# Attention scores of two heads on 64 rows of the array each, in a fused attention and mixture-of-experts kernel

## The chip, the cores and the metric

One core of one Trainium2 chip runs the whole program. The metric is device time in microseconds (us). A profile is one execution; its span runs from the first to the last instruction.

## The reference

Block-causal attention (batch 4, 8 heads, 576 positions, head size 64, blocks of 64), and then four dense experts over the 2304 tokens:

```python
scores = scale * np.matmul(q, k.transpose(0, 1, 3, 2))
scores = np.where(block_i >= block_j, scores, -1000000000.0)   # blocks of 64
attn = np.exp(scores - np.max(scores, axis=-1, keepdims=True))
attn = attn / (np.sum(attn, axis=-1, keepdims=True) + 1e-09)
x = np.matmul(attn, v)             # then (B, S, H * D) as 2304 x 512
...
for e in range(E):                 # E = 4, w1[e] 512 x 1024, w2[e] 1024 x 512
    h = np.maximum(x @ w1[e], 0.0)
    out += p[:, e:e + 1] * (h @ w2[e])
```

## The kernel before, in words

**The experts.** The tokens are in five blocks: the first 64 positions of the four batches (256 tokens), and then positions 64 to 576 of each batch (512 tokens each). A block takes 32 chunks (expert, 128 hidden columns); a chunk is 12 products `h` (`mm1`, L961) and 6 or 12 products `acc` (`mm2`, L1006). All are fp32r products; each fp32 operand is split into a rounded high part and the low rest (`w1h` and `w1l`, `xh` and `xl`, `hh` and `hl`), and three products (high by high, high by low, low by high) stand for one.

**The attention** of batches 0 to 3 runs ahead of their blocks in units of two heads (`unit`). The four units of batch 0 are "plain": fp32 products of whole K and Q (L510), each head on its own 64 rows of the array. The twelve units of batches 1 to 3 are "split" units. In one of these K of both heads is transposed (`kT`), and for each head `KK` gets the high part on 64 partitions and the low part on the other 64 (two copies and two differences, with the columns rotated for the second head, so that the corner's stand side by side). Q is loaded twice, once for each half of the partitions, side by side for the heads (1024 columns), transposed (`qT`), and split into `HH` and `LL`. One product of `KK` with `HH` (L522) and one with `LL` (L523) then contract over all 128 rows, for every piece of keys: 512, 448, 320 and 192 query columns per head, and a corner of 64 keys for both heads together (L568, L569, 128 columns).

The products of a piece go to a PSUM tile `att` of 512 columns, of which there are two. They are emptied by a copy to `S` and running maxima into `cm`; GpSimd finds the maxima over the keys (`mx`), ScalarE takes exp, and `S` is split into `PH` and `PL` for the products with V (L723), of which the corner's (`VJ`) is fp32.

**The order** of all instructions is made while the program is built: `Flow.run` plays threads of operations against estimated costs, and takes the operation that can start first. `late` adds 1500 ns (`LAG`) to what a score product waits for. Expert products fill what is free on TensorE.

Of the kernel before, what the change touches and what calls it, by code (L numbers as in the profile page):

```python
# [206 lines left out]
def kernel(  # L207
# [60 lines left out]
    bufs("qr", 1, [P, 2 * MAXW])  # L268
    bufs("vr", 1, [P, MAXT, 2, D])
    bufs("kT", 1, [P, S])  # L270
    bufs("qT", 1, [P, 2 * MAXW])
    bufs("KK", 2, [P, 2 * S], F32R)
    bufs("HH", 1, [P, 2 * MAXW], F32R)
    bufs("LL", 1, [P, 2 * MAXW], F32R)
    bufs("VS", 2, [P, MAXT, 4, D], F32R)
    bufs("VJ", 2, [P, 2, 3, D])
# [24 lines left out]
    bufs("st", 4, [P, 32])  # L301
    ident = const.tile([P, P], F32, name="ident")
# [67 lines left out]
    def unit(u, ua, us, ju, pu, ph, job, dst, c):  # L370
# [13 lines left out]
        def k_thread():  # L384
# [33 lines left out]
        def q_thread():  # L418
            yield ("until", lambda: now[0] >= gate[u])
            yield ("until", lambda: started())  # L420
            qr = yield fl.take("qr", ua)
            vals = []
            for h, j in ((h, j) for h in range(2) for j in range(2 if plain else 4)):
                p0, c0 = (64 * h + 32 * j, 0) if plain else (32 * j, h * W)
                vals.append((yield dma(
                    qr.tile[p0:p0 + 32, c0:c0 + W].rearrange("c (i r) -> c i r", r=32),
                    q[b, h0 + h, q0:q1, 32 * (j % 2):32 * (j % 2) + 32].rearrange("(i c) r -> c i r", c=32),
                    W * 128, u=[qr], prio=pr)))
            yield ("until", lambda: left_first[0] == 0)
            qT = yield fl.take("qT", ua)  # L430
            n = W if plain else 2 * W
            t = yield op("dve", 1.04 * n + 70, lambda _: nc.vector.transpose(out=qT.tile[:, :n], in_=qr.tile[:, :n]),
                         vals, [qr, qT], pr)
            fl.give(qr)
            if plain:
                st["q"] = (qT, t)
                return
            HH = yield fl.take("HH", us)
            LL = yield fl.take("LL", us)
            a = yield a_copy(HH.tile[:, :2 * W], qT.tile[:, :2 * W], 2 * W, [t], [qT, HH], pr)  # L440
            l = yield tt(BOTH, LL.tile[:, :2 * W], qT.tile[:, :2 * W], HH.tile[:, :2 * W], SUB, 2 * W, [a], [qT, HH, LL], pr)
            fl.give(qT)
            st["q"] = (HH, LL, a, l)

        def v_thread():
# [12 lines left out]
            for h in range(2):  # L458
                if odd:
                    jv.append((yield dma(VJ.tile[64 * h:64 * h + 64, VJ.tile.shape[1] - 1, 1, :], v[b, h0 + h, q1 - MASK_BLOCK:q1], 64 * 256,  # L460
                                         u=[VJ], prio=pr + 0.005)))
# [26 lines left out]
        if plain:  # L488
            banks.sort(key=lambda x: (x[1][0][0], x[0]))
# [3 lines left out]
        def s_thread():  # L493
# [8 lines left out]
            if plain:  # L502
                qT, qv = st["q"]
                Q = [qT]
                need = lambda h: ka + [qv]
                cost = lambda w: 2 * max(107.0, 2 * w / 2.4 + 2.5)

                def product(o, h, k0, n, lo):
                    hp = slice(64 * h, 64 * h + 64)
                    nc.tensor.matmul(out=o, lhsT=KK.tile[hp, k0:k0 + n], rhs=qT.tile[hp, lo:W], start=True, stop=True)  # L510
            else:
                HH, LL, qa, ql = st["q"]
                Q = [HH, LL]
                Hv = HH.tile[:, :2 * W].rearrange("p (h w) -> p h w", h=2)
                Lv = LL.tile[:, :2 * W].rearrange("p (h w) -> p h w", h=2)
                need = lambda h: (ka + kb if h is None else kb if h else ka) + [qa, ql]
                cost = lambda w: 2 * max(85.0, w / 2.4 + PEO)

                def product(o, h, k0, n, lo):
                    at = k0 + (q1 + MASK_BLOCK * odd) * h  # L520
                    hs = h
                    nc.tensor.matmul(out=o, lhsT=KK.tile[:, at:at + n], rhs=Hv[:, hs, lo:W], start=True, stop=False)  # L522
                    nc.tensor.matmul(out=o, lhsT=KK.tile[:, at:at + n], rhs=Lv[:, hs, lo:W], start=False, stop=True)  # L523

            for h, ps_list in banks:
                if plain and h is not None:

                    if h:
                        continue
                    two = []  # L530
                    for _ in range(2):
                        two.append((yield fl.take("att", None, bank_tag)))

                    def fn(_, two=two, ps_list=ps_list):
                        at = 0
                        for j, a, w, _ in ps_list:
                            for g in range(2):
                                product(two[g].tile[:, at:at + w], g, P * j, P, a - q0)
                            at += w

                    ws = [x[2] for x in ps_list]
                    m = yield op("pe", 300.0 + (2 * sum(ws) + ws[0] - sum(abs(x - y) for x, y in zip(ws, ws[1:]))) / 1.2,
                                 fn, need(0), [*two, KK] + Q, pr)
                    for g in range(2):
                        done, at = [m], 0
                        for j, a, w, _ in ps_list:
                            if a == P * j:
                                done.append((yield op("dve", 75.0, lambda _, ps=two[g].tile, x=at: nc.vector.memset(
                                    ps[64:128, x:x + 64], neg), [m], [two[g]], pr)))
                            at += w  # L550
                        st["banks"].append((g, ps_list, two[g], done))
                    continue
                pb = yield fl.take("att", None, bank_tag)
                ps = pb.tile
                use = [pb, KK] + Q
                done = []
                if h is None:
                    lo = W - MASK_BLOCK
                    n = 2 * MASK_BLOCK

                    def fn(_, ps=ps, n=n, lo=lo):
                        if plain:
                            for g in range(2):
                                r = slice(64 * g, 64 * g + 64)
                                product(ps[r, r], g, q1 - MASK_BLOCK, MASK_BLOCK, lo)
                        else:
                            lhsT = KK.tile[:, q1 - MASK_BLOCK:q1 + MASK_BLOCK]
                            nc.tensor.matmul(out=ps[:, :n], lhsT=lhsT, rhs=Hv[:, :, lo:W], start=True, stop=False)  # L568
                            nc.tensor.matmul(out=ps[:, :n], lhsT=lhsT, rhs=Lv[:, :, lo:W], start=False, stop=True)  # L569

                    m = yield late(op("pe", 220.0, fn, need(None), use, pr), lag)
                    m1 = yield op("dve", 75.0, lambda _, ps=ps: nc.vector.memset(ps[64:128, 0:64], neg), [m], [pb], pr)
                    m2 = yield op("dve", 75.0, lambda _, ps=ps: nc.vector.memset(ps[0:64, 64:128], neg), [m], [pb], pr)
                    done = [m, m1, m2]
                else:
                    at = 0
                    corners = []
                    for j, a, w, _ in ps_list:

                        def fn(_, o=ps[:, at:at + w], j=j, h=h, a=a):  # L580
                            product(o, h, P * j, P, a - q0)

                        m = yield late(op("pe", cost(w), fn, need(h), use, pr), lag)
                        done = [m]
                        if a == P * j:
                            corners.append(at)
                        at += w
                    for x in corners:
                        done.append((yield op("dve", 75.0, lambda _, ps=ps, x=x: nc.vector.memset(ps[64:128, x:x + 64], neg),  # L589
                                              done[:1], [pb], pr)))  # L590
                st["banks"].append((h, ps_list, pb, done))
            fl.give(KK, *Q)

# [535 lines left out]
```

## Time and profile before

| | us |
|---|---|
| median of 3 runs (935.1 to 936.45) | 935.82 |
| the profiled execution | 934.92 |
| its span | 933.1 |
| TensorE (PE) busy | 922.1 |
| VectorE (DVE) busy | 727.8 |
| ScalarE (ACT) busy | 424.2 |
| GpSimd (POOL) busy | 140.6 |

The span leaves out 1.8 us of the execution's own time. PE is TensorE's matmuls and PEld its weight loads, which run beside them. A matmul's time in a row reaches to its modelled end, and matmuls are pipelined, so the cost of one in a stream is the step from its start to the start of the next. The chain that ended last gives such steps.

### The profile page before, as it was taken

The page shows a single profiled execution, that of the slowest core. Times are in us where ns is not written, and L with a number is a line of the kernel's source. Part 1 is how long each engine was busy: PE and PEld are TensorE (multiplying, and loading weights), DVE is VectorE, ACT ScalarE, POOL GpSimd, SP SyncE. Part 2 cuts the span into 40 slices and gives each one's busy share as a digit, 9 for nine tenths or more (in the row PEclk, how much of TensorE's full clock was granted, in tenths as well). Part 3 has the DMA queues.
Part 4 walks back from the last instruction along what each step waited for, and adds up shares of the span by engine and source line. Part 5 has one row for each costly group of instructions (what it writes and reads, how often), then busy time and mean ns, then how long its engine had stood idle before and what let it go on. Part 6 is the DMA issues. An engine that isn't in the chain of part 4 may idle for free.

```text
span 933.1 us, 12703 instructions
## 1 busy us (share of the span) xinstructions
PE 922.1 (99%) x4381; PEld 759.0 (81%) x4382; DVE 727.8 (78%) x1323; ACT 424.2 (45%) x726; POOL 140.6 (15%) x59
## 2 busy tenths in 40 slices
PE   8999999999999999999999999999999999999998
PEld 4777787888888888888888888888888888888886
DVE  6888879788998988878998889898987754545442
ACT  3477656645565445436454545454434322222220
POOL 2101100131212121212122202112121200000000
PEclk9999999999999999999999999999999999999999
DMA  9765447625352355452523546343523343333311
GB/s 167 169 172 149 125 144 177 160 69 138 89 133 77 102 131 152 97 128 79 142 69 99 127 125 161 100 107 113 116 84 88 99 148 98 95 101 92 100 57 45
DMA packets 235648, 107.83 MB, mean 116 GB/s; under 512 B 130880, under 2 KB 212800, under 8 KB 235584
## 3 DMA queue, kind: packets, MB, share of 16 engines
q1 hardware_dynamic: 232416, 106.24, 43.0%
q10 hardware_dynamic: 3168, 0.79, 0.5%
q8 instruction: 34, 0.56, 0.3%
q14 instruction: 30, 0.25, 0.1%
HBM read 102.27 MB, written 4.72 MB: 115 GB/s over the span
## 4 chain that ended last, share of the span: by engine, by line
PE 94%; DVE 2%; DMA 2%; ACT 1%; SPq 1%; issue 1%; DVEq 0%; ACTq 0%
PE h L961 42%; PE acc L1006 41%; PE att L723 5%; PE att L523 2%; PE att L522 2%; PE acc L723 1%; SPq L320 1%; DMA S<-in_k_dram 0%; DMA w2r<-in_moe_w_dram 0%; PE att L510 0%; DVE cm L333 0%; DMA kr<-in_k_dram 0%; DMA w1r<-in_moe_w_dram 0%; DVE o L1035 0%; PE acc L510 0%
## 5 line engine op out<-in xcount | busy, mean ns | idle before, releaser
L961 PE MATMUL h<-xh,w1h 128*128 128x512 f32 (+1 forms) x640 | 239.1, 374 | 0.6 <-ACT w1h L326 0.6
L961 PE MATMUL h<-xh,w1l 128*128 128x512 f32 (+1 forms) x640 | 236.1, 369 | 1.4 <-DVE w1l L333 1.4
L961 PE MATMUL h<-xl,w1h 128*128 128x512 f32 (+1 forms) x640 | 235.7, 368 | 0.0
L1006 PE MATMUL acc<-w2h,hh 128*128 128x512 f32 x576 | 226.3, 393 | 0.0
L1006 PE MATMUL acc<-w2l,hh 128*128 128x512 f32 x576 | 224.8, 390 | 0.0
L1006 PE MATMUL acc<-w2h,hl 128*128 128x512 f32 x576 | 224.5, 390 | 0.0
L978 ACT ACTIVATE hh<-h 128x512 fp32r<-128x512 f32 (+1 forms) x160 | 88.9, 556 | 206.9 <-PE h L961 204.1
L326 ACT CAST w2h<-w2r 128x512 fp32r<-128x512 f32 x153 | 95.1, 621 | 151.7 <-PE acc L1006 149.1
L333 DVE TENSOR_TENSOR w2l<-w2r,w2h 128x512 fp32r<-128x512 f32 x160 | 109.8, 686 | 53.3 <-ACT w2h L326 52.9
L961 PEld LDWEIGHTS h<-xh,w1h 128*128 128x128 f32 x640 | 120.7, 189 | 22.9 <-issue 2.2
L961 PEld LDWEIGHTS h<-xh,w1l 128*128 128x128 f32 x640 | 120.5, 188 | 22.3 <-DVE w1l L333 2.0
L961 PEld LDWEIGHTS h<-xl,w1h 128*128 128x128 f32 x640 | 120.7, 189 | 19.5 <-DVE xl L333 0.2
L980 DVE SCALAR_TENSOR_TENSOR hl<-h,hh 128x512 fp32r<-128x512 f32 (+1 forms) x160 | 100.8, 630 | 36.4 <-ACT hh L978 35.4
L1006 PEld LDWEIGHTS acc<-w2h,hl 128*128 128x128 f32 x576 | 108.2, 188 | 22.9
L1006 PEld LDWEIGHTS acc<-w2h,hh 128*128 128x128 f32 x576 | 108.3, 188 | 21.2 <-ACT w2h L326 0.7
L1006 PEld LDWEIGHTS acc<-w2l,hh 128*128 128x128 f32 x576 | 108.4, 188 | 20.1
L333 DVE TENSOR_TENSOR w1l<-w1r,w1h 128x512 fp32r<-128x512 f32 x160 | 114.4, 715 | 9.6 <-ACT w1h L326 5.9
L680 POOL PARTITION_ALL_REDUCE S<-S x24 | 81.3, 3437 | 240.2 <-DVE S L333 174.0
L644 POOL PARTITION_ALL_REDUCE mx<-cm x16 | 54.5, 3407 | 358.5 <-DVE cm L333 279.3
L326 ACT CAST w1h<-w1r 128x512 fp32r<-128x512 f32 x115 | 71.2, 619 | 16.7 <-DMA w1r<-in_moe_w_dram 16.4
L326 ACT COPY S<-att 128x512 f32<-128x512 f32 (+2 forms) x88 | 47.5, 540 | 54.5 <-DVE att L589 31.9
L333 DVE TENSOR_TENSOR S<-S,mx 128x1024 f32<-128x1024 f32 (+4 forms) x80 | 60.3, 791 | 4.0 <-POOL mx L644 4.0
(130 smaller groups left out, 855.5 us busy)
## 6 DMA issues: line engine op xcount, KB each, us to landing
w1r<-in_moe_w_dram SPq DMA_DIRECT2D x160, 256.0 KB, 2.9
w2r<-in_moe_w_dram SPq DMA_DIRECT2D x160, 256.0 KB, 2.8
qr<-in_q_dram SPq DMA_DIRECT2D x112, 64.0 KB, 2.3
kr<-in_k_dram SPq DMA_DIRECT2D x64, 72.0 KB, 2.9
out_dram<-o SPq DMA_DIRECT2D x16, 256.0 KB, 2.4
vr<-in_v_dram SPq DMA_DIRECT2D x24, 128.0 KB, 2.6
VN<-in_v_dram SPq DMA_DIRECT2D x8, 128.0 KB, 2.8
S<-in_k_dram SPq DMA_DIRECT2D x4, 128.0 KB, 4.6
```

What stands on the lines that cost most here:

```text
L320: o = op(q, 550.0, lambda e: (nc.sync if e == "sp" else nc.scalar).dma_start(out=dst, in_=src), r, u, prio)
L326: o = op(engs, 0, lambda e: nc.scalar.copy(dst, src) if e == "act" else nc.vector.tensor_copy(dst, src), r, u, prio)
L333: o = op(engs, 0, lambda e: ENG[e].tensor_tensor(out=dst, in0=a, in1=b, op=alu), r, u, prio)
L522: nc.tensor.matmul(out=o, lhsT=KK.tile[:, at:at + n], rhs=Hv[:, hs, lo:W], start=True, stop=False)
L523: nc.tensor.matmul(out=o, lhsT=KK.tile[:, at:at + n], rhs=Lv[:, hs, lo:W], start=False, stop=True)
L644: lambda _: nc.gpsimd.partition_all_reduce(mx.tile[:, :2 * W], src, P, RED.max),
L680: st["sums"].append((yield op("pool", 150 + 6.3 * W, lambda _, h=h: nc.gpsimd.partition_all_reduce(Sv[:, h, W:2 * W], Sv[:, h, :W], P, RED ...
L723: nc.tensor.matmul(out=o, lhsT=lhsT, rhs=rhs, start=(i == 0), stop=(i == n - 1))
L961: nc.tensor.matmul(out=ps[:, :n], lhsT=s.tile[:, ks], rhs=x.tile[:, kc, :n], start=(kc == 0 and m == 0), stop=(kc == KC - 1 and m == 2),)
L978: a = yield op("act", 0.833 * n + 55, lambda _: nc.scalar.activation(hh.tile[:, :n], ps[:, :n], AF.Relu), [mm], [pb, hh], 0.0)
L980: l = yield op("dve", 1.04 * n + 70, lambda _: nc.vector.scalar_tensor_tensor(out=hl.tile[:, :n], in0=ps[:, :n], scalar=0.0, in1=hh.tile[: ...
L1006: nc.tensor.matmul(out=acc, lhsT=s.tile[:, ts], rhs=w.tile, start=(f == 0 and m == 0), stop=(f == FC - 1 and m == 2))
```

## The change

In the split units K of both heads is split by one copy and one difference over 128 partitions: high parts in the first half of `KK`'s columns, low parts in the second. Q is loaded once (four transfers in place of eight), and transposed and split with 512 columns in place of 1024. Each piece is then computed by three products per head (high by high, low by high, high by low), each over 64 rows: head 0 on rows 0 to 63, head 1 on rows 64 to 127, in turns, into two `att` tiles that are taken together. `plain` units use the same code with one term. The corner takes three products over 128 rows, of 128 keys with `ZZ`, which holds Q's corner of head 0 on the upper rows, of head 1 on the lower, and nil elsewhere; two more DVE products with `diag` make it. The 64 keys too many are masked by one memset, and meet rows of `VJ` that are nil.

```diff
...
-            a1 = yield a_copy(kk[0:64, :q1], kt[0:64, :q1], q1, [t], [kT, KK], pr)
-            l1 = yield tt(BOTH, kk[64:128, :q1], kt[0:64, :q1], kk[0:64, :q1], SUB, q1, [a1], [kT, KK], pr)
-            rot = MASK_BLOCK * odd
-            second = []
-            for to, of, n in ((q1 + rot, 0, q1 - rot), (q1, q1 - rot, rot)):
-                if n:
-                    second.append((yield a_copy(kk[64:128, to:to + n], kt[64:128, of:of + n], n, [t], [kT, KK], pr)))
-                    second.append((yield tt(BOTH, kk[0:64, to:to + n], kt[64:128, of:of + n], kk[64:128, to:to + n],
-                                            SUB, n, second[-1:], [kT, KK], pr)))
+            a = yield a_copy(kk[:, :q1], kt[:, :q1], q1, [t], [kT, KK], pr)
+            l = yield tt(BOTH, kk[:, S:S + q1], kt[:, :q1], kk[:, :q1], SUB, q1, [a], [kT, KK], pr)
             fl.give(kT)
-            st["k"] = (KK, [a1, l1], second)
+            st["k"] = (KK, [a], [l])
...
-            for h, j in ((h, j) for h in range(2) for j in range(2 if plain else 4)):
-                p0, c0 = (64 * h + 32 * j, 0) if plain else (32 * j, h * W)
+            for h, j in ((h, j) for h in range(2) for j in range(2)):
+                p0 = 64 * h + 32 * j
...
-            a = yield a_copy(HH.tile[:, :2 * W], qT.tile[:, :2 * W], 2 * W, [t], [qT, HH], pr)
-            l = yield tt(BOTH, LL.tile[:, :2 * W], qT.tile[:, :2 * W], HH.tile[:, :2 * W], SUB, 2 * W, [a], [qT, HH, LL], pr)
+            a = yield a_copy(HH.tile[:, :W], qT.tile[:, :W], W, [t], [qT, HH], pr)
+            l = yield tt(BOTH, LL.tile[:, :W], qT.tile[:, :W], HH.tile[:, :W], SUB, W, [a], [qT, HH, LL], pr)
             fl.give(qT)
-            st["q"] = (HH, LL, a, l)
+            Z, zs = [], []
+            for x in (HH, LL):
+                z = yield fl.take("ZZ")
+                zs.append((yield tt("dve", z.tile, x.tile[:, W - MASK_BLOCK:W].unsqueeze(1).to_broadcast([P, 2, MASK_BLOCK]),
+                                    diag, MUL, 2 * MASK_BLOCK, [a, l], [x, z], pr)))
+                Z.append(z)
+            st["q"] = (HH, LL, Z, [a, l], zs)
...
+                    n_ = VJ.tile.shape[1] - 1
+                    at = VJ.tile[64 * h:64 * h + 64, n_, 1, :] if plain else VJ.tile[64:128, n_, 2 * h, :]
...
-                HH, LL, qa, ql = st["q"]
-                Q = [HH, LL]
-                Hv = HH.tile[:, :2 * W].rearrange("p (h w) -> p h w", h=2)
-                Lv = LL.tile[:, :2 * W].rearrange("p (h w) -> p h w", h=2)
-                need = lambda h: (ka + kb if h is None else kb if h else ka) + [qa, ql]
-                cost = lambda w: 2 * max(85.0, w / 2.4 + PEO)
-                def product(o, h, k0, n, lo):
-                    at = k0 + (q1 + MASK_BLOCK * odd) * h
-                    hs = h
-                    nc.tensor.matmul(out=o, lhsT=KK.tile[:, at:at + n], rhs=Hv[:, hs, lo:W], start=True, stop=False)
-                    nc.tensor.matmul(out=o, lhsT=KK.tile[:, at:at + n], rhs=Lv[:, hs, lo:W], start=False, stop=True)
+                HH, LL, Z, qv, zv = st["q"]
+                Q, terms, dep = [HH, LL], [(0, HH), (S, HH), (0, LL)], ka + kb + qv
+            def products(outs, k0, n, lo):
+                for i, (at, x) in enumerate(terms):
+                    for g, o in enumerate(outs):
+                        hp = slice(64 * g, 64 * g + 64)
+                        a = at + k0
+                        nc.tensor.matmul(out=o, lhsT=KK.tile[hp, a:a + n], rhs=x.tile[hp, lo:W],
+                                         start=(i == 0), stop=(i == len(terms) - 1))
+            def cost(ws):
+                if plain:
+                    return 300.0 + (2 * sum(ws) + ws[0] - sum(abs(x - y) for x, y in zip(ws, ws[1:]))) / 1.2
+                return 200.0 + sum(3 * (w / 2.4 + 2 * PEO) for w in ws)
...
+                two = []
+                for _ in range(1 if h is None else 2):
+                    two.append((yield fl.take("att", None, bank_tag)))
+                ps = two[0].tile
+                def fn(_, h=h, two=two, ps_list=ps_list):
+                    at = 0
+                    for j, a, w, _ in ps_list:
+                        if h is None and plain:
+                            products([two[0].tile[r:r + 64, r:r + 64] for r in (0, 64)], q1 - MASK_BLOCK, MASK_BLOCK, W - MASK_BLOCK)
+                        elif h is None:
+                            for i, (at, x) in enumerate(((0, Z[0]), (S, Z[0]), (0, Z[1]))):
+                                nc.tensor.matmul(out=two[0].tile[:, :P], lhsT=KK.tile[:, at + q1 - P:at + q1],
+                                                 rhs=x.tile.rearrange("p h w -> p (h w)"), start=(i == 0), stop=(i == 2))
+                        else:
+                            products([x.tile[:, at:at + w] for x in two], P * j, P, a - q0)
+                        at += w
+                ws = [x[2] for x in ps_list]
+                if h is None and not plain:
+                    m = yield late(op("pe", 3 * (P / 2.4 + PEO), fn, dep + zv, [*two, KK, *Z], pr), lag)
+                else:
+                    m = yield late(op("pe", cost(ws), fn, dep, [*two, KK] + Q, pr), lag)
...
+                    for r in ((ps[64:128, 0:64], ps[0:64, 64:128]) if plain else (ps[0:64, 0:128],)):
...
+                    nc.gpsimd.memset(b.tile, 0.0)
...
+            nc.gpsimd.memset(diag[64 * g:64 * g + 64, g, :], 1.0)
+            nc.gpsimd.memset(diag[64 * g:64 * g + 64, 1 - g, :], 0.0)
...
```

On PE, before, the first split unit begins with two products of 512 columns and two of 448 for head 0 (`att_127` and `att_128` are the two PSUM tiles, the numbers those of buffers; `HH` and `LL` are Q's parts):

```order
L961 MATMUL h_121<-xh_90,w1h_61 128x512
L961 MATMUL h_121<-xl_92,w1h_61 128x512
L961 MATMUL h_121<-xh_90,w1l_65 128x512
L522 MATMUL att_127<-HH_101,KK_99 128x512
L523 MATMUL att_127<-LL_102,KK_99 128x512
L522 MATMUL att_128<-HH_101,KK_99 128x448
L523 MATMUL att_128<-LL_102,KK_99 128x448
L961 MATMUL h_121<-xh_90,w1h_61 128x512
L961 MATMUL h_121<-xl_92,w1h_61 128x512
L961 MATMUL h_121<-xh_90,w1l_65 128x512
```

After, on PE at the same place, both tiles are filled at once, by six products of 64 rows:

```order
L980 MATMUL acc_124<-w2l_74,hh_82 128x512
L980 MATMUL acc_124<-w2h_70,hl_84 128x512
L516 MATMUL att_128<-HH_101,KK_99 128x512
L516 MATMUL att_127<-HH_101,KK_99 128x512
L516 MATMUL att_128<-HH_101,KK_99 128x512
L516 MATMUL att_127<-HH_101,KK_99 128x512
L516 MATMUL att_128<-LL_102,KK_99 128x512
L516 MATMUL att_127<-LL_102,KK_99 128x512
L935 MATMUL h_122<-xh_89,w1h_64 128x256
L935 MATMUL h_122<-xl_91,w1h_64 128x256
```

The 448-column pieces, which followed at once before, now come 18 expert products later, when both tiles are empty again. The other split units show the same four stretches (512; 448; 320 with 192; corner).

On PE the corner of that unit, before:

```order
L961 MATMUL h_121<-xl_92,w1h_63 128x512
L961 MATMUL h_121<-xh_90,w1l_67 128x512
L568 MATMUL att_127<-HH_101,KK_99 128x128
L569 MATMUL att_127<-LL_102,KK_99 128x128
L961 MATMUL h_121<-xh_90,w1h_63 128x512
L961 MATMUL h_121<-xl_92,w1h_63 128x512
L961 MATMUL h_121<-xh_90,w1l_67 128x512
```

and after:

```order
L980 MATMUL acc_126<-w2l_73,hh_81 128x512
L980 MATMUL acc_126<-w2h_69,hl_83 128x512
L540 MATMUL att_128<-ZZ_133,KK_99 128x128 x2
L540 MATMUL att_128<-ZZ_134,KK_99 128x128
L935 MATMUL h_121<-xh_90,w1h_63 128x512
L935 MATMUL h_121<-xl_92,w1h_63 128x512
L935 MATMUL h_121<-xh_90,w1l_67 128x512
```

It has three products of 128 columns in place of two.

On DVE, before, the work for the first split unit stands ahead of the expert weights' low parts (`w1l_65` is the first that block 1 needs):

```order
L398 STREAM_TRANSPOSE kT_97<-kr_93 128x576
L333 TENSOR_TENSOR KK_99<-kT_97,KK_99 64x576
L333 TENSOR_TENSOR KK_99<-kT_97,KK_99 64x512
L980 SCALAR_TENSOR_TENSOR hl_83<-h_121,hh_81 128x256
L333 TENSOR_TENSOR KK_99<-kT_97,KK_99 64x64
L432 STREAM_TRANSPOSE qT_98<-qr_95 128x1024
L326 CAST HH_101<-qT_98 128x1024
L980 SCALAR_TENSOR_TENSOR hl_84<-h_122,hh_82 128x256
L333 TENSOR_TENSOR LL_102<-qT_98,HH_101 128x1024
L333 TENSOR_TENSOR VS_103<-vr_96,VS_103 128x4x128
L333 TENSOR_TENSOR w1l_65<-w1r_77,w1h_61 128x512
L333 TENSOR_TENSOR w2l_73<-w2r_79,w2h_69 128x512
```

and after:

```order
L400 STREAM_TRANSPOSE kT_97<-kr_93 128x576
L954 SCALAR_TENSOR_TENSOR hl_84<-h_122,hh_82 128x256
L426 STREAM_TRANSPOSE qT_98<-qr_95 128x512
L335 TENSOR_TENSOR KK_99<-kT_97,KK_99 128x576
L335 TENSOR_TENSOR LL_102<-qT_98,HH_101 128x512
L335 TENSOR_TENSOR VS_103<-vr_96,VS_103 128x4x128
L954 SCALAR_TENSOR_TENSOR hl_83<-h_121,hh_81 128x256
L335 TENSOR_TENSOR ZZ_133<-HH_101,diag 128x128
L335 TENSOR_TENSOR w1l_68<-w1r_78,w1h_64 128x512
L335 TENSOR_TENSOR ZZ_134<-LL_102,diag 128x128
L335 TENSOR_TENSOR w2l_76<-w2r_80,w2h_72 128x512
L335 TENSOR_TENSOR w1l_65<-w1r_77,w1h_61 128x512
```

Three differences of K have become one, Q's operations have half the columns and its cast has left DVE, and two `ZZ` products have come in.

## Rows read from the trace of the kernel before

**Rows 1.** The page: busy time by engine; the chain that ended last.

```profile
PE 922.1 (99%) x4381; PEld 759.0 (81%) x4382; DVE 727.8 (78%) x1323; ACT 424.2 (45%) x726; POOL 140.6 (15%) x59
...
PE 94%; DVE 2%; DMA 2%; ACT 1%; SPq 1%; issue 1%; DVEq 0%; ACTq 0%
```

**Rows 2.** Busy time by stretch: stretch, length, engines, granted clock, DMA.

```profile
270.00:390.00 120.00, 120.00 (x556) 100.50 (x555) 104.81 (x179) 62.11 (x100) 26.38 (x8) 1.00 0.43 114
```

**Rows 3.** The chain, 150 to 200 us: start, us, what.

```profile
160.29 2.72 PE h L961 x12
...
165.05 0.20 PE att L522
...
166.15 0.14 PE att L522
166.29 0.15 PE att L523
166.44 0.09 PE att L522
166.53 0.11 PE att L523
166.64 2.09 PE h L961 x9
168.73 0.06 PE att L568
168.79 0.11 PE att L569
168.90 0.74 PE h L961 x3
```

**Rows 4.** Groups by line and form: busy us, mean ns, idle before.

```profile
L326 ACT COPY S<-att 128x512 f32<-128x512 f32 x56 | 32.9, 587 | 38.3 <-DVE att L589 21.4 <-PE att L523 11.2 <-PE h L961 4.4
...
L522 PE MATMUL att<-HH,KK 128*128 128x512 f32 x24 | 9.4, 393 | 0.0
```

**Rows 5.** TensorE's timeline, a plain unit's scores: start, us, instruction, count.

```profile
28.91 0.28 PE L961 MATMUL h<-xl,w1h 128*128 128x256 f32 x1
29.03 0.28 PE L961 MATMUL h<-xh,w1l 128*128 128x256 f32 x1
29.24 0.53 PE L510 MATMUL acc<-qT,kT 64*128 64x320 f32 x1
29.24 0.53 PE L510 MATMUL att<-qT,kT 64*128 64x320 f32 x1
29.61 0.43 PE L510 MATMUL acc<-qT,kT 64*128 64x320 f32 x1
...
30.05 0.32 PE L510 MATMUL att<-qT,kT 64*128 64x192 f32 x1
30.30 0.50 PE L1006 MATMUL acc<-w2h,hh 128*128 128x512 f32 x1
30.64 0.40 PE L1006 MATMUL acc<-w2l,hh 128*128 128x512 f32 x1
```

**Rows 6.** Weight loads of the same stretch.

```profile
29.24 0.18 PEld L510 LDWEIGHTS att<-qT,kT 64*128 64x128 f32 x1
29.34 0.19 PEld L510 LDWEIGHTS acc<-qT,kT 64*128 64x128 f32 x1
```

**Rows 7.** TensorE's timeline, into a plain unit's products with V.

```profile
50.44 0.39 PE L1006 MATMUL acc<-w2h,hl 128*128 128x512 f32 x1
50.67 0.59 PE L723 MATMUL acc<-S,VN 128*128 128x512 f32 x1
```

**Rows 8.** TensorE's timeline, ahead of the first split unit.

```profile
154.49 0.50 PE L961 MATMUL h<-xh,w1l 128*128 128x512 f32 x1 [1.14 <-DVE w1l L333]
```

**Rows 9.** VectorE's timeline, the same stretch.

```profile
152.01 1.22 DVE L333 TENSOR_TENSOR LL<-qT,HH 128x1024 fp32r<-128x1024 f32 x1
...
153.75 0.68 DVE L333 TENSOR_TENSOR w1l<-w1r,w1h 128x512 fp32r<-128x512 f32 x1
```

More of the change, by code (lines that the diff above doesn't have):

```diff
@@ L267 @@
     bufs("kr", 2, [P, S])
-    bufs("qr", 1, [P, 2 * MAXW])
+    bufs("qr", 1, [P, MAXW])
     bufs("vr", 1, [P, MAXT, 2, D])
     bufs("kT", 1, [P, S])
-    bufs("qT", 1, [P, 2 * MAXW])
+    bufs("qT", 1, [P, MAXW])
     bufs("KK", 2, [P, 2 * S], F32R)
-    bufs("HH", 1, [P, 2 * MAXW], F32R)
-    bufs("LL", 1, [P, 2 * MAXW], F32R)
+    bufs("HH", 1, [P, MAXW], F32R)
+    bufs("LL", 1, [P, MAXW], F32R)
     bufs("VS", 2, [P, MAXT, 4, D], F32R)
-    bufs("VJ", 2, [P, 2, 3, D])
+    bufs("VJ", 2, [P, 1, 3, D])
     bufs("VN", 2, [P, (MASK_BLOCK + MAXW) // P + 1, 3, D])
@@ L301 @@
     bufs("st", 4, [P, 32])
+    bufs("ZZ", 2, [P, 2, MASK_BLOCK], F32R)
+    diag = const.tile([P, 2, MASK_BLOCK], F32, name="diag")
     ident = const.tile([P, P], F32, name="ident")
@@ L422, in q_thread @@
             vals = []
-            for h, j in ((h, j) for h in range(2) for j in range(2 if plain else 4)):
-                p0, c0 = (64 * h + 32 * j, 0) if plain else (32 * j, h * W)
+            for h, j in ((h, j) for h in range(2) for j in range(2)):
+                p0 = 64 * h + 32 * j
                 vals.append((yield dma(
-                    qr.tile[p0:p0 + 32, c0:c0 + W].rearrange("c (i r) -> c i r", r=32),
-                    q[b, h0 + h, q0:q1, 32 * (j % 2):32 * (j % 2) + 32].rearrange("(i c) r -> c i r", c=32),
+                    qr.tile[p0:p0 + 32, :W].rearrange("c (i r) -> c i r", r=32),
+                    q[b, h0 + h, q0:q1, 32 * j:32 * j + 32].rearrange("(i c) r -> c i r", c=32),
                     W * 128, u=[qr], prio=pr)))
@@ L430, in q_thread @@
             qT = yield fl.take("qT", ua)
-            n = W if plain else 2 * W
-            t = yield op("dve", 1.04 * n + 70, lambda _: nc.vector.transpose(out=qT.tile[:, :n], in_=qr.tile[:, :n]),
+            t = yield op("dve", 1.04 * W + 70, lambda _: nc.vector.transpose(out=qT.tile[:, :W], in_=qr.tile[:, :W]),
                          vals, [qr, qT], pr)
@@ L459, in v_thread @@
                 if odd:
-                    jv.append((yield dma(VJ.tile[64 * h:64 * h + 64, VJ.tile.shape[1] - 1, 1, :], v[b, h0 + h, q1 - MASK_BLOCK:q1], 64 * 256,
+                    n_ = VJ.tile.shape[1] - 1
+                    at = VJ.tile[64 * h:64 * h + 64, n_, 1, :] if plain else VJ.tile[64:128, n_, 2 * h, :]
+                    jv.append((yield dma(at, v[b, h0 + h, q1 - MASK_BLOCK:q1], 64 * 256,
                                          u=[VJ], prio=pr + 0.005)))
@@ L487, in unit @@
                 banks.append((h, cur))
-        if plain:
-            banks.sort(key=lambda x: (x[1][0][0], x[0]))
+        banks.sort(key=lambda x: (x[1][0][0], x[0]))
         if odd:
@@ L525, in s_thread @@
-            for h, ps_list in banks:
[L526 to L551, printed above, removed]
-                    continue
[L553 to L556, printed above, removed]
-                if h is None:
[L558 to L577, printed above, removed]
@@ new lines, in s_thread @@
+                Q, terms, dep = [qT], [(0, qT)], ka + [qv]
+            else:
+                HH, LL, Z, qv, zv = st["q"]
[7 more added lines that the diff above has]
+                                         start=(i == 0), stop=(i == len(terms) - 1))
@@ new lines, in cost @@
+            def cost(ws):
+                if plain:
+                    return 300.0 + (2 * sum(ws) + ws[0] - sum(abs(x - y) for x, y in zip(ws, ws[1:]))) / 1.2
+                return 200.0 + sum(3 * (w / 2.4 + 2 * PEO) for w in ws)
+            for h, ps_list in banks:
+                if h:
+                    continue
+                two = []
[19 more added lines that the diff above has]
+                    m = yield late(op("pe", cost(ws), fn, dep, [*two, KK] + Q, pr), lag)
+                if h is None:
+                    done = [m]
+                    for r in ((ps[64:128, 0:64], ps[0:64, 64:128]) if plain else (ps[0:64, 0:128],)):
+                        done.append((yield op("dve", 75.0, lambda _, r=r: nc.vector.memset(r, neg), [m], two, pr)))
+                    st["banks"].append((h, ps_list, two[0], done))
+                    continue
+                for g in range(2):
+                    done, at = [m], 0
@@ L578, in s_thread @@
                     for j, a, w, _ in ps_list:
[L580 to L584, printed above, removed]
                         if a == P * j:
-                            corners.append(at)
+                            done.append((yield op("dve", 75.0, lambda _, ps=two[g].tile, x=at: nc.vector.memset(
+                                ps[64:128, x:x + 64], neg), [m], [two[g]], pr)))
@@ L587, in s_thread @@
                         at += w
[L588 to L592, printed above, removed]
+                    st["banks"].append((g, ps_list, two[g], done))
+            fl.give(KK, *Q, *([] if plain else Z))
         def e_thread():
@@ L717, in pv_flow @@
                         nj = VJ.tile.shape[1] - 1
-                        lhsT = VJ.tile[:, j - narrow[0][0], h:h + 2, :] if j is not None else VJ.tile[:, nj, 1 - h:3 - h, :]
+                        g = h if j is not None or not plain else 1 - h
+                        lhsT = VJ.tile[:, j - narrow[0][0] if j is not None else nj, g:g + 2, :]
                         cost, dv, c1 = 2 * max(107.0, 2 * w / 2.4 + 2.5), jv, h * C + c0
@@ L1096 @@
             for b in fl.free[tag]:
-                n, x = b.tile.shape[1] - 1, 1.0 if tag == "VN" else 0.0
-                nc.gpsimd.memset(b.tile[:, :n, 1, :], x)
-                nc.gpsimd.memset(b.tile[:, n, 0:3:2, :], x)
+                if tag == "VJ":
+                    nc.gpsimd.memset(b.tile, 0.0)
+                    continue
+                n = b.tile.shape[1] - 1
+                nc.gpsimd.memset(b.tile[:, :n, 1, :], 1.0)
+                nc.gpsimd.memset(b.tile[:, n, 0:3:2, :], 1.0)
+        for g in range(2):
+            nc.gpsimd.memset(diag[64 * g:64 * g + 64, g, :], 1.0)
+            nc.gpsimd.memset(diag[64 * g:64 * g + 64, 1 - g, :], 0.0)
         fl.run()
```

6 lines of the change are left out of this document (removed).

## The prediction

> **What bounds the kernel now.** I read the page first. TensorE is busy for 99% of the span, and 94% of the chain that ended last is its own work [rows 1]. From there I went to the stretches. In one of 120 us within the split units TensorE is busy for all 120.00 us at a granted clock of 1.00, while DVE has 104.81 us of work and ACT 62.11 [rows 2]. So whatever the change saves on DVE, ACT and the queues is worth nothing there, and every step that it adds on TensorE is paid in full. Third comes the chain, for the step that each product takes in the stream: an expert product of 512 columns takes 2.72/12 = 0.227 us, where 512 columns at 2.4 GHz are 0.213 [rows 3]. Fourth is the timeline of the plain units, the only place before the change where two heads compute on 64 rows each [rows 5, 6]. Last is the one large wait that split units leave on TensorE, 1.14 us for `w1l` ahead of the first of them [rows 8].
>
> **What a split unit costs before.** For one head: two products of 512 columns at an expert's step, 0.46 us; two of 448 at 0.20, so 0.40; the 320s 0.14 + 0.15, so 0.29; the 192s 0.09 + 0.11, so 0.20 [rows 3]. The nine expert products behind the 192s take 2.09 us where nine steps are 2.04, so 0.05 is left over. That is 1.40 us, and 2.80 for two heads; the groups have 24 of each form, two in each of 12 units [rows 4]. The corner takes 0.06 + 0.11, and the three expert products behind it 0.74 in place of 0.68, so 0.23. A unit has 3.03 us.
>
> **What it costs after.** *Columns.* Per piece three products of each head, the two heads at once if the halves work as in the plain units. There both halves start at 29.24, and again at 29.61 [rows 5]. The fp32 product of 320 columns passes four times, in two instructions of two passes: 320 x 2 / 2.4 GHz = 0.267, and from 29.61 to 30.05 the rows have 0.44 for 0.267 + 0.160. So two halves do run in the time of one. For fp32r a unit has 3 x 1472 columns = 1.84 us.
>
> *Going over to 64 rows and back.* This is the term that decides. The last expert product ahead of that stretch starts at 29.03, its step is 0.12 (28.91 to 29.03), so TensorE is free for the next at 29.15. The first halves start at 29.24, 0.09 late, and their step is 0.37 in place of 0.267, since their weights load only then (load and product both start at 29.24 [rows 6]). At the other end the last pair is over at 30.05 + 0.16 = 30.21; the expert product starts at 30.30 and has a step of 0.34 in place of 0.23. From 29.15 to 30.64 - 0.23 = 30.41 there are 1.26 us for 4 x 512 / 2.4 = 0.85 us of columns: 0.41 us for one trip [rows 5]. It isn't the change from fp32r to fp32: into the plain units' products with V, fp32 on all rows, TensorE goes in one usual step, 50.44 to 50.67 [rows 7]. A split unit makes three trips (512; 448; 320 with 192), for with two `att` tiles it can't fill the next pair before this one is empty: 1.23 us.
>
> *Steps.* In the full-row stream a product takes 0.013 us over its columns, in the plain pairs about 0.005 (0.44 against 0.427 over two steps). Twelve pairs: 0.06 to 0.16, none as the lowest. I take 0.08. The loads of one half follow one another at 0.10 us (29.24, 29.34 [rows 6]), and a 192-column pair lasts 0.08: two of three pairs wait 0.02, so 0.04.
>
> *Corner.* Its second product had a step of 0.11, bound by the load ahead of it, since 128 columns are 0.053; a third adds the same 0.11: 0.34. The Trainium skill ("TensorE: Matmul & The Clock Gate", section Back-to-back issue gap) gives some 81 ns for each 128-column product in a stream. By that the third would add 0.08, and the sum over twelve units be 0.4 us lower; the trace has 0.11 here, and I keep it.
>
> Sum of a unit: 1.84 + 1.23 + 0.08 + 0.04 + 0.34 = 3.53 us, 0.50 over before, and 6.0 us over twelve.
>
> **What else moves.** The wait of 1.14 us [rows 8]: `w1l` stands on DVE behind K's, Q's and V's splitting of the first unit, with `LL` alone at 1.22 us and `w1l` itself starting at 153.75 [rows 9]. After the change Q's transpose and `LL` have half the columns, three K differences are one, and Q's cast goes to ACT; two 128-column `ZZ` products come in, and the `w1l` in question is behind them. Halving `LL` alone takes off 0.6 us, the transpose of the same 1024 columns about as much, so I take the wait as gone: -1.1. (It may stay: 0.) What is late next there is the product itself. The other savings (four Q transfers less per unit, smaller copies and differences) lie under TensorE's full stretches and are worth 0. If that cover were gone, it would be because DVE fell behind; it has 13% to spare and gets less work. `ZZ` makes the corner wait for one DVE operation more, behind `LL`; the corner comes last of the four stretches, after tens of expert products, so 0. The new memsets at the start (`diag`, four of 64 x 64 on GpSimd) stand behind those that the first block needs and long before the first `ZZ`: 0. The corner's V goes to other partitions by the same two transfers: 0. The plain units' products are the same, in an order that shifts since their corner's planned cost rises; the number of trips is the same. I take 0, and 1 us either way, about one wait like that of [rows 8].
>
> 6.0 - 1.1 = +4.9. The profiled execution took 934.92 us (a span of 933.1 and 1.8 around it) and would take 939.8; it lies 0.9 under the median of the runs, 935.82, so the median becomes 940.7.
>
> **The rivals.**
>
> *Going over costs nothing for fp32r.* Then a unit has 1.84 + 0.16 + 0.04 + 0.34 = 2.38, 0.65 less than before: -7.8 and -1.1, so 926.9. The Trainium skill ("TensorEngine Tiling (Array Packing)", Theoretical Speedup) puts a contraction of 64 rows at two tiles and up to twice the speed, with no price for a trip; its Key Properties say that a change of mode drains TensorE, without a figure. The first alone would give this rival. Rows 5 speak against it with 0.41 us, and rows 7 against fp32 as its cause. 6%.
>
> *Half the price goes.* fp32r weights might be loaded ahead of the trip, and the long first steps vanish (0.10 + 0.11): 36 x 0.21 = 7.6 less, so 933.1, at the edge of no change. Against it: both ends of the plain stretch show the load starting with its product, and I see nothing in the weights' type that would alter that. 10%.
>
> *The halves don't overlap in one-pass products.* fp32 asks for each column twice, fp32r for a new one in every cycle from both halves. If these take turns, a unit has 1.84 us more: +22.1, 962.8. Nothing in the rows shows such a limit, and none excludes it. 7%.
>
> *The trip waits for empty tiles (slower by more).* Each pair now needs both `att` tiles; before, one was filled while the other was emptied. In the new order 9 of the 12 448-column pairs come 12 expert products (2.72 us) behind the 512s. Meanwhile two copies of 0.59 [rows 4], the maxima and one chunk's relu have to be done. Copies and relu in a row leave about 0.7 us; one more operation ahead of them eats it. If those nine waited 0.59 each, +5.3: 946.0. It decides from the first such wait of half a microsecond on. For it: the one tile pair; against it: the planner keeps 1500 ns in hand, and the full stretch of [rows 2] has no wait by the same margin. 11%.
>
> **How the numbers follow.** 66% for the forecast, 940.7, whose own range is 937.5 to 943.5 (steps 0 to 0.16 a unit, -1 to +1; the wait of 1.14 gone or not; the plain units 1 either way). The range from 935 to 946 leaves out the two faster rivals (16%, less the upper part of the second) and the third, and takes most of the fourth. About 0.2%, 1.9 us, can be told from no change: faster is under 933.9, slower over 937.7. Faster has the first rival and half of the second, 0.11; no change the other half and the low end of the forecast, 0.11; slower the rest, 0.78.
>
> **What would show it.** In the profile after: pairs of score products over 64 rows that start within 0.01 us of each other, 0.22 to 0.23 apart at 512 columns; an expert product on either side with 0.09 us of gap and a first step 0.10 too long, 36 times; the 192 pairs 0.10 apart; corner steps of 0.06, 0.11, 0.11; no wait of 1 us for `w1l` near the first split unit; TensorE full in the middle. I am wrong if a trip costs under 0.25 us, if the halves start one after the other, or if TensorE waits for `att` to be emptied.

## The result, and the profile after

| | before | after |
|---|---|---|
| median of 6 runs, us | 935.18 | 941.09 |
| span of the profiled execution, us | 933.1 | 938.5 |
| PE busy, us | 922.1 | 928.6 |
| DVE busy, us | 727.8 | 694.7 |

The ratio is 1.0061 (95% interval 1.0047 to 1.0075): slower by 5.9 us in the medians, 5.4 in the spans. The forecast was +4.9 and 940.7. One of the six executions after the change took 5279.01 us; the ratio leaves it out, and without it the median is 941.05.

The page after, busy time by engine and the chain's shares, against [rows 1]:

```profile
PE 928.6 (99%) x4489; PEld 749.9 (80%) x4490; DVE 694.7 (74%) x1300; ACT 416.0 (44%) x713; POOL 139.1 (15%) x61
...
PE 96%; DMA 2%; SPq 1%; DVE 1%; ACT 0%; issue 0%
```

And the stretch of [rows 2]:

```profile
270.00:390.00 120.00, 120.00 (x569) 97.83 (x568) 99.02 (x176) 56.40 (x91) 22.25 (x8) 1.00 0.39 105
```

DVE has 33 us less to do, and TensorE is as full as it was: what DVE gave back in this stretch was not what TensorE waited for. TensorE's timeline of one trip after the change (two matmuls of the same name are merged; start, us):

```profile
292.23 0.39 PE L980 MATMUL acc<-w2h,hl 128*128 128x512 f32 x1
292.55 0.67 PE L516 MATMUL att<-HH,KK 64*128 64x448 f32 x4
293.06 0.36 PE L516 MATMUL att<-LL,KK 64*128 64x448 f32 x2
293.35 0.50 PE L980 MATMUL acc<-w2h,hh 128*128 128x512 f32 x1
293.68 0.39 PE L980 MATMUL acc<-w2l,hh 128*128 128x512 f32 x1
```

It reads like [rows 5]. The expert product that starts at 292.23 leaves TensorE free at 292.46. The halves start 0.09 later; three pairs later, at 293.06 + 0.20 = 293.26, they are through; the expert product starts 0.09 after that, and its step is 0.33 in place of 0.23. From 292.46 to 293.68 - 0.23 = 293.45 there are 0.99 us for 3 x 448 columns, 0.56 us: 0.43 on top. The first weight loads start with the first products, and not ahead of them:

```profile
292.55 0.30 PEld L516 LDWEIGHTS att<-HH,KK 64*128 64x128 f32 x4 [0.35 <-issue]
```

The corner, against the last rows of [rows 3]:

```profile
210.62 0.45 PE L540 MATMUL att<-ZZ,KK 128*128 128x128 f32 x3
210.91 0.45 PE L935 MATMUL h<-xh,w1h 128*128 128x512 f32 x1
211.19 0.40 PE L935 MATMUL h<-xl,w1h 128*128 128x512 f32 x1
```

Three corner products take 0.29 us and lengthen the next step to 0.28, 0.34 in all as forecast.

Measured in this way at every stretch (starts of the expert products around it, less their usual steps; mean over the 12 units), the 512s cost 1.09 us, the 448s 1.00, the 320s with the 192s 1.15, the corner 0.34: 3.58 us a unit, where before it was 3.02. Twelve times 0.56 are 6.8 us. The waits of 0.31 and 1.14 us ahead of the first split unit [rows 8 has the longer] are gone: -1.45. That makes +5.3, and the start of the last stretch in the chain of work that ended last agrees. Before, and after:

```profile
923.15 3.41 PE acc L1006 x15
```

```profile
929.12 3.42 PE acc L980 x15
```

It is 5.97 us later. Of this 0.61 was there ahead of all split units (the expert product that is the last before the first of them after the change starts at 149.70 in place of 149.09), which leaves 5.36. What follows the last stretch is 0.6 us shorter after the change, hence 5.4 in the spans. The 0.61 are the sum of larger things in the first stage. The first expert product starts 1.4 us earlier, and the first plain corner then waits longer:

```profile
32.76 0.48 PE L516 MATMUL att<-qT,kT 64*64 64x64 f32 x4 [2.31 <-DVE cm L335]
33.17 0.79 PE L980 MATMUL acc<-w2h,hh 128*128 128x512 f32 x1
33.76 0.63 PE L980 MATMUL acc<-w2l,hh 128*128 128x512 f32 x1
34.19 0.63 PE L980 MATMUL acc<-w2h,hl 128*128 128x512 f32 x1
```

Behind the wait of 2.31 us (1.20 before) the steps are 0.43 us where 0.23 is usual (33.76 to 34.19): TensorE runs at 1.2 in place of 2.4 GHz, and the granted clock of the stretch from 24 to 60 us is 0.95.

### The profile page after: what moved, and what is told of

It reads as the page before. It is cut to its first block, busy times and chain, and to the rows that moved or that the text cites. A ratio compares the mean times of both kernels' runs of the same rounds, so it can differ in the third digit from the quotient of the medians.

```text
span 938.5 us, 12820 instructions
## 1 busy us (share of the span) xinstructions
PE 928.6 (99%) x4489; PEld 749.9 (80%) x4490; DVE 694.7 (74%) x1300; ACT 416.0 (44%) x713; POOL 139.1 (15%) x61
## 4 chain that ended last, share of the span: by engine, by line
PE 96%; DMA 2%; SPq 1%; DVE 1%; ACT 0%; issue 0%
PE h L935 42%; PE acc L980 42%; PE att L697 5%; PE att L516 4%; PE acc L697 1%; SPq L322 1%; DMA w1r<-in_moe_w_dram 1%; DMA S<-in_v_dram 1%; DMA w2r<-in_moe_w_dram 0%; PE att L540 0%; PE acc L516 0%; DMA S<-in_k_dram 0%; DVE o L1009 0%; DVE w1l L335 0%; ACT w2h L328 0%
## 5 line engine op out<-in xcount | busy, mean ns | idle before, releaser
L980 PE MATMUL acc<-w2h,hh 128*128 128x512 f32 x576 | 229.5, 398 | 0.0
L328 ACT CAST w2h<-w2r 128x512 fp32r<-128x512 f32 x156 | 97.1, 622 | 158.9 <-PE acc L980 155.6
L335 DVE TENSOR_TENSOR w1l<-w1r,w1h 128x512 fp32r<-128x512 f32 x160 | 111.5, 697 | 9.9 <-ACT w1h L328 6.2
```

Source lines behind the costliest of these rows:

```text
L328: o = op(engs, 0, lambda e: nc.scalar.copy(dst, src) if e == "act" else nc.vector.tensor_copy(dst, src), r, u, prio)
L335: o = op(engs, 0, lambda e: ENG[e].tensor_tensor(out=dst, in0=a, in1=b, op=alu), r, u, prio)
L980: nc.tensor.matmul(out=acc, lhsT=s.tile[:, ts], rhs=w.tile, start=(f == 0 and m == 0), stop=(f == FC - 1 and m == 2))
```

## The experiments

**One trip in place of three.** In the split units all pieces are issued at once into the same two tiles:

```diff
+                first = h is not None and ps_list[0][0] == 0
+                if plain or h is None or first:
+                    two = []
...
+                    if first and not plain:
+                        for _, more in [x for x in banks if x[0] == 0][1:]:
+                            at = 0
+                            for j, a, w, _ in more:
+                                products([x.tile[:, at:at + w] for x in two], P * j, P, a - q0)
+                                at += w
...
```

> The changed kernel with the same score products, but the three stretches of a unit (512; 448; 320 with 192) issued one behind the other into the same two PSUM tiles, so that the later pieces overwrite the earlier ones and what is copied out of the tiles is not the scores; the copies and maxima are the same in number and size. A unit goes to 64 rows once in place of three times. My theory (a trip to 64 rows and back costs 0.41 to 0.45 us whatever is computed in it): 24 trips fewer, 9.6 us off the changed kernel's 941.1, so about 931.5, and 1.15 us less per unit on TensorE for the three stretches taken together, no: 0.8 us less per unit (3.24 to about 2.45). Rival (products on half the rows are slow in themselves, by some 0.1 us a pair, and a trip costs nothing): the pairs are all still there, 941 within 1 us.

Measured: 931.42 us, ratio to before 0.9961 (0.9946 to 0.9976), 9.7 below the changed kernel. The timeline of one unit:

```profile
284.58 0.39 PE L990 MATMUL acc<-w2h,hl 128*128 128x512 f32 x1
284.90 0.73 PE L516 MATMUL att<-HH,KK 64*128 64x512 f32 x4
285.46 0.40 PE L516 MATMUL att<-LL,KK 64*128 64x512 f32 x2
285.70 0.57 PE L516 MATMUL att<-HH,KK 64*128 64x448 f32 x4
286.11 0.36 PE L516 MATMUL att<-LL,KK 64*128 64x448 f32 x2
286.31 0.46 PE L516 MATMUL att<-HH,KK 64*128 64x320 f32 x4
286.60 0.31 PE L516 MATMUL att<-LL,KK 64*128 64x320 f32 x2
286.75 0.36 PE L516 MATMUL att<-HH,KK 64*128 64x192 f32 x4
286.95 0.28 PE L516 MATMUL att<-LL,KK 64*128 64x192 f32 x2
287.15 0.50 PE L945 MATMUL h<-xh,w1h 128*128 128x512 f32 x1
287.49 0.39 PE L945 MATMUL h<-xl,w1h 128*128 128x512 f32 x1
```

The same 24 products take 2.46 us where three trips had 3.24. With 1.84 us of columns in both, 0.62 = one trip + the steps and 1.40 = three trips + the steps: a trip is 0.39 us, and all that the steps take on top 0.23. With two of the three trips gone the change would have been a gain. The time adds up in this trace too: from the last expert product ahead of the split units to the start of the last stretch there are 770.48 us (150.29 to 920.77) in place of 779.42, 8.9 less. The units give 12 x 0.78 = 9.4, and three corners that take 0.55 to 0.59 us in place of 0.34 take 0.7 back, which leaves 8.7.

**More trips, and a control.** Products whose results nobody reads were added at two places of a unit. In one kernel some of them use all 128 rows:

```diff
                             products([x.tile[:, at:at + w] for x in two], P * j, P, a - q0)
                         at += w
+                        if h is not None and not plain and w in (448, 320):
+                            x0 = at
+                            nc.tensor.matmul(out=two[0].tile[:, x0:x0 + 64], lhsT=KK.tile[:, 0:P], rhs=HH.tile[:, 0:64],
+                                             start=True, stop=True)
...
```

In the control a pair of products on 64 rows each stands in their place; both have one more such pair behind the 448s.

> The changed kernel with products added whose results nobody reads: behind the 448-column pairs one product of 64 columns on all 128 rows and then one pair of 64 columns on 64 rows; between the 320s and the 192s one product of 64 columns on all rows. That is two more trips a unit, 24 in all. My theory: 24 x (0.41 to 0.46) and 12 pairs of about 0.10, so +11 to +12.5 over the changed kernel, some 953. Rival (a trip costs nothing): the extra columns alone, 36 x 0.1 = about +3.6 at most, like the next kernel.

> Control of the kernel with full-row products in between: the same places and columns, but all the added products are pairs of 64 columns on 64 rows each, so there is no further trip. Both theories: 36 pairs, each bound by its weight load of 0.10 us, +3.6 over the changed kernel at most, about 944.5. My theory puts the kernel with full-row products 8 to 9 us above this one; the rival puts the two level.

Measured: 952.48 us (ratio 1.0185, 1.0170 to 1.0200) and 944.76 (1.0101, 1.0086 to 1.0116). The kernel with full-row products takes 11.4 us more than the changed kernel, the control 3.7 more, 0.10 for each of its 36 pairs. So the full-row products cost 7.7 us more than the pairs in their place, 0.32 us for each of 24, and each of them brings two changes of mode. In the timeline of the first:

```profile
296.13 0.38 PE L516 MATMUL att<-LL,KK 64*128 64x448 f32 x2
296.44 0.30 PE L547 MATMUL att<-HH,KK 128*128 128x64 f32 x1
296.67 0.30 PE L552 MATMUL att<-HH,KK 64*128 64x64 f32 x2
296.90 0.50 PE L989 MATMUL acc<-w2h,hh 128*128 128x512 f32 x1
```

64 columns are 0.027 us, and each change holds up the next product by 0.2: 296.44, 296.67, 296.90. Between the 320s and the 192s the full-row product stands in alone:

```profile
300.88 0.39 PE L989 MATMUL acc<-w2h,hl 128*128 128x512 f32 x1
...
301.83 0.30 PE L547 MATMUL att<-HH,KK 128*128 128x64 f32 x1
...
302.90 0.39 PE L989 MATMUL acc<-w2l,hh 128*128 128x512 f32 x1
```

Measured as above, this stretch takes 1.57 us in every unit where the changed kernel has 1.15. Of the 0.42, 0.03 are columns, which leaves 0.39 for the trip, as in the one-trip kernel. The rival that a trip costs nothing is out, from both sides.

**Heads not in turns.**

```diff
-                for i, (at, x) in enumerate(terms):
-                    for g, o in enumerate(outs):
+                for g, o in enumerate(outs):
+                    for i, (at, x) in enumerate(terms):
```

> The changed kernel with the two heads' products not in turns: all three of head 0 and then all three of head 1, for each piece. If products start strictly in the order of the program, only the last of head 0 and the first of head 1 run together: five steps in place of three, 2 x 1472 columns / 2.4 GHz x 12 units = +14.7, about 956. If the queue finds the other half's products by itself (in the plain units, whose heads stand one behind the other, both halves started together): no change, 941.

Measured: 940.76 us (ratio 1.0064, 1.0047 to 1.0081), the changed kernel's time. TensorE's timeline, what starts between 292.50 and 292.60 us, where the 448s begin:

```profile
292.54 0.48 PE L516 MATMUL att<-HH,KK 64*128 64x448 f32 x2
```

Two products start within 0.01 us of each other, though in the kernel two more of head 0's stand between head 0's first and head 1's first. The row names no head, but the whole stretch takes 1.01 us, against 1.00 in the changed kernel, and two steps more of 448 columns would be 0.37. So the overlap of the halves needs no turns: head 1's products pass head 0's, which stand ahead of them. (The third rival, halves that take turns, was out with the changed kernel: its three pairs of 448 columns take 0.71 us, 292.55 to 293.26, where six products one after the other are 1.12 us of columns alone.)

**The old preparation under the new products.** K in three copies and three differences, Q with 1024 columns:

```diff
-            a = yield a_copy(kk[:, :q1], kt[:, :q1], q1, [t], [kT, KK], pr)
+            for r, to, n in ((slice(0, 64), 0, q1), (slice(64, 128), 0, q1 - MASK_BLOCK), (slice(64, 128), q1 - MASK_BLOCK, MASK_BLOCK)):
+                a.append((yield a_copy(kk[r, to:to + n], kt[r, to:to + n], n, [t], [kT, KK], pr)))
...
-            a = yield a_copy(HH.tile[:, :W], qT.tile[:, :W], W, [t], [qT, HH], pr)
+            a = yield a_copy(HH.tile[:, :2 * W], qT.tile[:, :2 * W], 2 * W, [t], [qT, HH], pr)
...
```

> The products of the change alone: K and Q are prepared in the pieces and sizes of the kernel before (K by three copies and three differences, Q loaded, transposed and split with 1024 columns, of which the second half is a copy that nothing reads), the score products and the corner are those of the change. My theory: preparation lies under TensorE's full stretches and counts only ahead of the first split unit, where it may bring back the waits of 0.31 and 1.14 us: 941.1 to 942.5. Rival (the lighter preparation is worth something all along, DVE being 80% busy): more than 2 us above the changed kernel, over 943.

Measured: 947.38 us (ratio 1.0131, 1.0113 to 1.0149), 6.3 above the changed kernel. I expected 1.4 at most, and that was wrong. TensorE's timeline ahead of the first split unit:

```profile
152.39 0.39 PE L938 MATMUL h<-xh,w1h 128*128 128x256 f32 x1 [1.34 <-ACT w1h L328]
152.61 0.28 PE L938 MATMUL h<-xl,w1h 128*128 128x256 f32 x1
153.73 0.58 PE L938 MATMUL h<-xh,w1l 128*128 128x256 f32 x1 [0.84 <-DVE w1l L335]
...
158.33 0.63 PE L983 MATMUL acc<-w2l,hh 128*128 128x512 f32 x1
158.75 0.63 PE L983 MATMUL acc<-w2h,hl 128*128 128x512 f32 x1
```

The waits are back, 2.18 us in sum, and behind them the steps are 0.43 us again: half clock until 160 us, a granted clock of 0.67 from 150 to 160, which costs at most 3.3 us. Later there are single waits of 1.36 and 0.66 us, which the changed kernel has not. But this is the trace of the slowest of the four executions: 950.06 us, with a mean granted clock of 0.995. The other three took 945.99 to 947.82 us at 0.998, where the changed kernel has 0.997 to 0.998. By this they were no longer at half clock than the changed kernel, and are still 4.9 to 6.7 us slower. So the half clock is not what makes up the 6.3; the four waits, which the changed kernel has not, are 4.2 in sum, and where the rest lies is not shown.

**More time for it.** A unit begins 6 chunks ahead in place of 4, under the old preparation and under the light one:

```diff
-LEAD, MARGIN = 4.0, 4.0
+LEAD, MARGIN = 6.0, 4.0
```

> The products of the change with the preparation in the pieces and sizes of the kernel before, as in the kernel that took 947.4 us, and units begun 6 chunks ahead in place of 4. If the 6 us that the old preparation cost there are waits of TensorE from too much work on DVE and ACT in too little time ahead of the first split unit (1.34 and 0.84 us, and the half clock behind them), more time takes most of them off: 941 to 943.5. If the heavier preparation costs TensorE something all along, it stays near 947.

> The changed kernel with units begun 6 chunks ahead in place of 4. The light preparation has no wait left there to take away, so 941.1 within 1 us, while the same edit took 2.9 us off the kernel before; the trips are the same 36. If the edit gains the same 2.9 us here, it works by something other than that wait.

Measured: 945.99 us with the old preparation (ratio 1.0118, 1.0102 to 1.0134), 940.18 with the light one (1.0062, 1.0050 to 1.0075). The second came as expected. The first did not: its ratio can't be told from the 1.0131 without the edit, and the two waits ahead of the first split unit only moved ahead with the work.

```profile
147.44 0.39 PE L938 MATMUL h<-xh,w1h 128*128 128x256 f32 x1 [1.20 <-ACT w1h L328]
147.66 0.28 PE L938 MATMUL h<-xl,w1h 128*128 128x256 f32 x1
148.86 0.58 PE L938 MATMUL h<-xh,w1l 128*128 128x256 f32 x1 [0.92 <-DVE w1l L335]
```

The two later waits are gone; from 150 us on TensorE is full. This too is the trace of the slowest of its executions (948.30 us, of 944.11 to 948.30).

**The kernel before with less waiting.** Three kernels: LAG for the plain units' scores too, LEAD of 6, and both:

```diff
-            lag = 0.0 if plain else LAG
+            lag = LAG
```

> The kernel before with one edit: score products of the plain units too get the 1500 ns of LAG, so that their planned start is later (the first plain corner comes 3 expert products later). My theory: takes part of the wait of 1.2 us ahead of the first plain corner, and with it the chance that the clock falls behind it: 0.4 to 1.5 us off, 934 to 935. Rival: the wait is for the weights' arrival and only moves to another product: 935.3.

> The kernel before with one edit: units may begin 6 chunks ahead of their stretch in place of 4 (LEAD). Tests whether the waits of 0.31 and 1.14 us ahead of the first split unit are a matter of too much preparation in too little time, which the change takes away too: my theory 1.4 us off, about 933.9. Rival (the waits move with the preparation): 935.3.

> The kernel before with both edits, LAG for the plain units' scores and units begun 6 chunks ahead. My theory: both gains add up, 1.5 to 3 us off, 932.5 to 933.8, under both kernels. Rival: nothing in sum, 935.3.

Measured: 934.72 us (ratio 0.9992, 0.9983 to 1.0001), 932.66 (0.9967, 0.9954 to 0.9979) and 932.49 (0.9967, 0.9955 to 0.9979). LAG alone can't be told from nothing. LEAD of 6 takes 2.9 us off, twice what I gave it. From 150 to 270 us TensorE is then full, where before it was 118.55 of 120 us. Before, and with LEAD of 6:

```profile
150.00:270.00 120.00, 118.55 (x550) 98.78 (x549) 104.94 (x189) 64.31 (x109) 23.89 (x7) 1.00 0.49 124
```

```profile
150.00:270.00 120.00, 120.00 (x560) 100.62 (x559) 108.33 (x194) 64.75 (x107) 24.67 (x7) 1.00 0.48 124
```

That is the 1.45 us of the two waits; the rest of the 2.9 I did not trace to its place. These two, with the full-row products of before, are faster than the kernel before and the changed one.

## Why the prediction was right

- *What bounds the kernel.* Right: TensorE's stream, to the end. 33 us less on DVE gained nothing in the full stretches, and the added 6.8 us came out in whole.
- *The trip.* Forecast at 0.41 us from the plain units, measured at 0.39 in the one-trip kernel; 36 of them are 14 us. The gaps of 0.09 and the long first steps stand at both ends. That fp32r would load ahead (the second rival) did not show: the loads start with their products.
- *Columns of both halves at once.* Right: 1.84 us a unit, and without turns too.
- *Steps and loads.* Here the size was off: 0.12 us a unit forecast (0.08 + 0.04), 0.23 measured. The one-trip timeline has 0.23 from pair to pair at 512 columns and 0.20 at 448, the full-row stream's steps, where I had gone halfway to the fp32 pairs'. Twelve times 0.11 are 1.3 us; the trips, 0.02 cheaper each, give 0.7 of it back. That is most of what the units' sum (+6.0 forecast, +6.8 measured, with before at 3.02 in place of 3.03) was short. (The two loads that the prediction reads from [rows 6] are of different heads; in the trace each half's second load does start 0.11 us behind its first.)
- *The corner.* Right, 0.34 us.
- *The wait for `w1l`.* Gone, with the 0.31 us ahead of it that I had not counted: -1.45 in place of -1.1.
- *The plain units.* "1 us either way" held in sum, +0.6, but it hides an earlier start, a longer wait at the corner and some 3 us at half clock, none of which I had named.
- *Waits for empty tiles.* None: the 448s take 1.00 us in every unit. The margin was larger than I put it: by the groups' means, two copies of 0.59 and a relu of 0.60 leave 0.9 of the 2.72 us, not 0.7.
- *What the light preparation is worth.* I put it at the one wait. Under the new products the old preparation costs 6.3 us: 4.2 us of waits in its one trace, in part far behind the first split unit, and more that no trace places. My sum was not touched by this, for the change took the waits away; the reasoning that lighter work under a full TensorE is worth 0 elsewhere was wrong for that kernel. That too little time was the cause of the first two waits fell with the first of the two LEAD kernels. Why the same preparation made the kernel before wait for 1.45 us only stays open; the planner places `w1h` and Q's cast on other engines there, the kernel with the old preparation makes `ZZ` on top (DVE 735.7 us, more than both kernels), and neither was tried apart.
- *The sum.* 6.8 - 1.45 + 0.61 is 5.96, where I had 4.9: 1.0 too little. That 940.7 lies only 0.4 from the measured 941.09 is luck: I added to 935.82, the median known then, and over all runs the kernel before has 935.18.

## What to carry to other kernels

Products on half the rows save columns, but every passage from full to half rows and back has a price of its own (0.39 us here): count the passages, and compare their price with the columns saved, before the products are split. Here a unit's pieces save 1472 columns, 0.61 us, and pay 1.17 us for the three passages that two PSUM tiles ask for. An existing use of the mode in the same trace, here the plain units, gave that price as 0.41, within 0.02 us. And work taken off an engine beside a full TensorE pays only where TensorE waits for it; but whether it waits has to be tried under the new products (the old preparation cost 1.45 us of waits under the old ones, 6.3 us under the new).

## What the hardware showed that was not expected

Products on different halves of the rows pass one another: with all of head 0's products ahead of head 1's in the kernel, the first two still start 0.01 us apart, and the time is the same (940.76 and 941.09 us).

The length of a wait alone did not decide whether TensorE went on at half clock. Eight of the kernels wait 2.03 to 2.56 us ahead of the first plain corner. In seven of them TensorE goes on at half clock, as in the rows of the changed kernel above. In the one-trip kernel they do not, and its granted clock is 1.00 from 24 to 60 us:

```profile
32.76 0.33 PE L516 MATMUL att<-qT,kT 64*64 64x64 f32 x4 [2.23 <-DVE cm L335]
33.02 0.50 PE L990 MATMUL acc<-w2h,hh 128*128 128x512 f32 x1
33.36 0.39 PE L990 MATMUL acc<-w2l,hh 128*128 128x512 f32 x1
33.59 0.40 PE L990 MATMUL acc<-w2h,hl 128*128 128x512 f32 x1
```

And in the kernel before with LEAD of 6 the half clock came at 24 us (0.95 granted in the same stretch), behind waits of at most 0.52 us since 15 us. What decides it these runs do not show.
